# One hand-written order for four engines against another: hashed attention and a channel mix on one core

## The chip, the cores and the metric

The kernel runs on one core of a Trainium2 chip. The metric is the device time of one execution in microseconds (us). A core has engines that work side by side, each through its own list of instructions and strictly in the order of that list: TensorE (PE in the profile, with PEld for its weight loads), VectorE (DVE), ScalarE (ACT), GpSimd (POOL), and SyncE (SP), whose list here holds the DMA transfers.

## What is computed

The reference is attention followed by a channel mix. Queries and keys are sorted into buckets by the signs of six projections, and a query attends only to keys of its own bucket:

```python
mask = q_bucket[:, :, :, None] == k_bucket[:, :, None, :]
scores = np.where(mask, scale * np.matmul(q, k.transpose(0, 1, 3, 2)), -1000000000.0)
scores = scores - np.max(scores, axis=-1, keepdims=True)
attn = np.exp(scores)
attn = attn / (np.sum(attn, axis=-1, keepdims=True) + 1e-09)
x = np.matmul(attn, v)                      # 4 batches, 8 heads, 768 rows, 64 wide
# ---- then, with the heads side by side (512 wide), x_prev = x one row later ----
xk = mu_k * x + (1.0 - mu_k) * x_prev
xr = mu_r * x + (1.0 - mu_r) * x_prev
k = np.maximum(xk @ w_k, 0.0)               # 512 -> 1024
out = 1.0 / (1.0 + np.exp(-(xr @ w_r))) * (k * k @ w_v)
```

## The kernel before

The 32 heads are taken two at a time: 16 pairs, four to a batch. The work is cut into 1348 operations, each a closure of one to a few dozen instructions. They are added pair by pair in the loop at the end of the function, numbered from 0 to 1347 as they are added, and then issued in the order of a list of numbers, `ORDER`. Which of the eight banks of PSUM an operation writes is read from a second list, `BANKS`. So both the order on each engine and the place of each intermediate result are written out by hand; only the order within one engine counts, and each engine waits by semaphores for what its next operation needs.

```python
    def schedule(self):
        self.slot = dict(zip(self.names, BANKS))
        return [self.ops[i] for i in ORDER]
```

Operations are named below as the code names them, with n the pair (0 to 15), b the batch and c a chunk of 128 rows:

- `ldq`, `ldv` (SP, L328 and L333): load q and k, or v, of a pair. `wl` and `wc` (SP L297, POOL L304): load a piece of the weights and cast it to bf16.
- `hi`, `lo` (DVE, L396 and L399): split q and k into two fp16 halves; from pair 4 on, one operation each for q and k together. `tr` (SP, L403): a DMA transpose of that result into `a`. The first two pairs use PE transposes instead.
- `bits` (PE, L423), `bx` (DVE, L426), four `row` operations (POOL, L443, one for q and k of each head): bucket signs, made into +-64, copied into `a` as six more rows of the product, so that one matrix product gives score and mask.
- `sc` (PE, L566): nine score steps of 1024 columns for each pair, each in two PSUM banks; `exp` (ACT, L570) takes a step out of PSUM and frees the banks.
- `vsum`, three steps (POOL, L354, L357, L360), `mean` (PE, L372 and L373), two `va` and one `mc` (DVE, L378 and L385): v less its mean, from pair 4 on.
- `oo` (PE, L593): attention times v, two heads of three groups each; `rc` and `ob` (DVE, L604 to L611): divide by the row sum. `ot`, `xt` (PE L621, DVE L624) or `otd` (SP, L627, a DMA transpose): turn the result round.
- `xs`, `xz`, `df`, `xka`, `xk`, `xra`, `xr` (DVE, L631 to L666): shift by a row and mix.
- For each batch: `kp` (PE, L681, 16 products), `relu` (ACT, L685, into one of four buffers `kr`), `sq` (DVE, L688, the square, which frees the `kr` buffer); `r` (PE, L701) and `tanh` (ACT, L704); `v` (PE, L714, two halves), `os` (DVE, L721) and the store `st` (SP, L724).

A warm-up of 24 small products on PE (`warm`, L250) fills the start.

Of the kernel before, what the change touches and what calls it, by code (L numbers as in the profile page):

```python
# [17 lines left out]
    1, 27, 33, 34, 36, 35, 30, 74, 72, 75, 73, 76, 77, 0, 2, 31, 28, 3, 4, 5, 6, 38, 7, 37, 91, 81, 82, 85, 100, 8, 9, 10, 11, 12, 13, 14,  # L18
    15, 16, 101, 17, 92, 119, 26, 102, 93, 120, 110, 103, 86, 118, 104, 111, 94, 105, 95, 78, 96, 121, 18, 113, 122, 123, 127, 97, 106, 107,
    128, 129, 187, 79, 112, 124, 98, 108, 135, 114, 99, 158, 19, 125, 20, 134, 115, 109, 136, 159, 156, 143, 116, 117, 193, 144, 29, 32, 39,  # L20
    40, 41, 42, 43, 44, 45, 46, 47, 80, 87, 88, 83, 84, 130, 131, 189, 132, 133, 242, 137, 196, 194, 157, 126, 138, 197, 186, 240, 239, 198,
    145, 162, 154, 152, 163, 89, 146, 155, 153, 168, 169, 195, 190, 147, 141, 139, 90, 142, 191, 246, 150, 140, 151, 164, 165, 166, 148, 21,
    149, 167, 247, 249, 188, 160, 209, 250, 161, 219, 170, 213, 248, 210, 251, 171, 172, 214, 220, 292, 293, 50, 48, 199, 192, 243, 215,
    216, 173, 244, 174, 200, 203, 299, 201, 22, 221, 300, 207, 23, 24, 25, 217, 222, 208, 202, 175, 176, 177, 245, 204, 205, 218, 262, 252,
    206, 263, 301, 211, 253, 178, 179, 52, 241, 452, 453, 454, 442, 228, 212, 443, 266, 229, 264, 267, 294, 265, 258, 230, 272, 56, 259,
    295, 296, 255, 254, 257, 297, 256, 54, 58, 223, 224, 225, 226, 231, 273, 232, 260, 268, 261, 227, 269, 270, 180, 233, 271, 181, 182,
    308, 309, 302, 51, 183, 234, 303, 49, 184, 314, 318, 235, 320, 236, 238, 53, 315, 305, 274, 306, 298, 304, 321, 319, 276, 281, 277, 282,
    322, 445, 275, 446, 307, 278, 279, 316, 237, 455, 323, 312, 317, 280, 324, 313, 456, 507, 325, 508, 331, 463, 464, 465, 332, 310, 466,
    333, 283, 284, 461, 334, 469, 311, 285, 473, 185, 335, 462, 470, 286, 447, 458, 460, 326, 474, 509, 327, 448, 475, 287, 449, 328, 467,
# [12 lines left out]
    753, 755, 549, 834, 601, 422, 783, 867, 550, 551, 426, 772, 835, 832, 833, 427, 836, 837, 814, 428, 815, 784, 785, 786, 656, 787, 602,
# [759 lines left out]
```

## Time and profile before

| what | us |
|---|---|
| median of 3 runs | 246.14 |
| lowest, highest of them | 245.51, 246.46 |
| the execution that was profiled | 245.97 |
| its span, from the first to the last instruction | 244.2 |
| PE, DVE, ACT and POOL busy in that span | 233.6, 191.8, 183.4, 96.4 |

The times inside the profile count from the start of the span, so 1.8 us of the profiled execution lie outside it. PE's time to the end of a product is modelled and takes in the pipeline, so a busy PE isn't one at its peak. A timeline row gives start, duration, engine, line, operation, output and input, and how many instructions were merged; in square brackets stands how long the engine was idle before them and what it waited for.

### The profile page before, as it was taken

Reading aid. Unit: us, or ns where it says so; the run is one execution under the profiler, and the core shown is the slowest. Engines: PE = TensorE matmul, PEld = TensorE weight load, DVE = VectorE, ACT = ScalarE, POOL = GpSimd, SP = SyncE. Lnnn points to the kernel's source line nnn. Section 1 sums busy time; section 2 is a strip of 40 time slices with the busy share of each in tenths; the row PEclk is TensorE's granted clock in tenths of the full one; section 3 lists DMA queues with packets and bytes.
Section 4 is the critical chain, followed back from the end, with each engine's and each line's share of the span. In section 5 each row is a group of like instructions: output and inputs, shape, how many; then the busy total and the mean of one; then the engine's idle time right before and its main releaser. Section 6 shows DMA issues by size and latency. Waiting matters only on the chain.

```text
span 244.2 us, 6300 instructions
## 1 busy us (share of the span) xinstructions
PE 233.6 (96%) x2533; PEld 146.4 (60%) x2550; DVE 191.8 (79%) x396; ACT 183.4 (75%) x242; POOL 96.4 (39%) x152
## 2 busy tenths in 40 slices
PE   8999999998999998999999999999999999999994
PEld 6885666575667546456555765556565665455443
DVE  5879698999999999999898989992368168965332
ACT  4699999899998676878769996678797881265410
POOL 6248977985369563556076320500450000000000
PEclk9999999999999999999999999999999999999999
DMA  6999999999999998998999779409112210103133
GB/s 212 376 273 217 228 211 246 349 185 328 267 283 232 281 305 212 203 260 224 317 154 206 112 164 177 131 17 225 57 34 91 73 35 34 54 1 116 57 132 129
DMA packets 72526, 44.01 MB, mean 180 GB/s; under 512 B 54832, under 2 KB 67504, under 8 KB 72496
## 3 DMA queue, kind: packets, MB, share of 16 engines
q1 hardware_dynamic: 72272, 43.40, 74.6%
q8 instruction: 20, 0.33, 0.6%
q10 hardware_dynamic: 224, 0.20, 0.2%
q14 instruction: 10, 0.08, 0.1%
HBM read 24.12 MB, written 6.29 MB: 125 GB/s over the span
## 4 chain that ended last, share of the span: by engine, by line
PE 67%; DVE 12%; DMA 11%; ACT 4%; issue 3%; POOL 1%; DVEq 0%
PE ps_all L566 16%; PE ps_all L714 14%; PE ps_all L681 14%; DMA a<-nh 11%; PE ps_all L593 7%; PE ps_all L701 7%; ACT pt L570 3%; PE ps_all L423 3%; DVE k L688 2%; PE ps_all L250 2%; POOL a L443 1%; DVE ob L611 1%; DVE va L378 1%; DVE bx L426 1%; PE ps_all L489 1%
## 5 line engine op out<-in xcount | busy, mean ns | idle before, releaser
L570 ACT ACTIVATE pt<-ps_all 128x1024 bf16<-128x1024 f32 x144 | 140.2, 1037 | 14.9 <-PE ps_all L566 13.9
L566 PE MATMUL ps_all<-a 128*128 128x256 f16 (+1 forms) x384 | 81.1, 325 | 2.5 <-DVE mc L385 0.8
L443 POOL COPY a<-bx 6x384 f32<-6x384 f32 x56 | 42.6, 761 | 41.8 <-DVE bx L426 23.9
L681 PE MATMUL ps_all<-xk,wk 128*128 128x384 bf16 x256 | 50.1, 326 | 0.5 <-ACT kr L685 0.5
L566 PEld LDWEIGHTS <-a 128*128 128x128 f16 x384 | 33.8, 98 | 25.6 <-issue 6.3
L593 PEld LDWEIGHTS <-pt 128*128 128x128 bf16 x1152 | 43.2, 97 | 9.1 <-issue 1.4
L714 PE MATMUL ps_all<-wv,k 128*128 128x512 bf16 (+2 forms) x199 | 46.1, 362 | 0.6
L593 PE MATMUL ps_all<-va,pt 128*128 128x65 bf16 x1152 | 45.6, 193 | 0.0
L688 DVE TENSOR_TENSOR k<-kr 128x384 bf16<-128x384 bf16 x64 | 27.5, 453 | 13.1 <-ACT kr L685 12.9
L685 ACT ACTIVATE kr<-ps_all 128x384 bf16<-128x384 f32 x64 | 30.0, 502 | 9.5 <-PE ps_all L681 6.4
L681 PEld LDWEIGHTS <-wk 128*128 128x128 bf16 x256 | 23.8, 98 | 17.5 <-issue 1.7
L704 ACT ACTIVATE rs<-ps_all 128x512 f32<-128x512 f32 x24 | 14.1, 597 | 26.5 <-PE ps_all L701 11.2
L714 PEld LDWEIGHTS <-k 128*128 128x128 bf16 x208 | 19.4, 98 | 18.4
L399 DVE SCALAR_TENSOR_TENSOR nh<-nat,nh 128x1536 f16<-128x1536 f32 (+1 forms) x16 | 26.4, 1652 | 0.3
L721 DVE SCALAR_TENSOR_TENSOR os<-rs,ps_all 128x512 f32<-128x512 f32 (+2 forms) x26 | 16.7, 641 | 11.5 <-PE ps_all L714 8.1
L701 PE MATMUL ps_all<-wr,xr 128*128 128x512 bf16 x88 | 23.1, 379 | 0.4
L354 POOL TENSOR_TENSOR vt<-vn 128x384 f32<-128x384 f32 x12 | 15.1, 1256 | 16.1 <-DMA vn<-in_v_dram 15.5
L611 DVE TENSOR_TENSOR ob<-ps_all,rc 128x384 bf16<-128x384 f32 x32 | 17.3, 550 | 0.4
L426 DVE TENSOR_SCALAR bx<-ps_all 128x768 uint16<-128x768 uint16 x14 | 13.4, 954 | 3.9 <-PE ps_all L423 3.6
L701 PEld LDWEIGHTS <-xr 128*128 128x128 bf16 x96 | 9.2, 98 | 9.7 <-issue 0.3
L396 DVE TENSOR_SCALAR nh<-nat 128x1536 f16<-128x1536 f32 (+1 forms) x16 | 14.7, 924 | 0.3 <-DMA nat<-in_k_dram 0.3
L378 DVE SCALAR_TENSOR_TENSOR va<-ps_all,vn 128x384 bf16<-128x384 f32 x24 | 12.7, 548 | 1.5 <-ACT kr L685 0.8
(86 smaller groups left out, 191.1 us busy)
## 6 DMA issues: line engine op xcount, KB each, us to landing
vn<-in_v_dram SPq DMA_DIRECT2D x16, 384.0 KB, 5.5
out_dram<-os SPq DMA_DIRECT2D x23, 256.0 KB, 2.3
nat<-in_q_dram SPq DMA_DIRECT2D x15, 384.0 KB, 4.9
nat<-in_k_dram SPq DMA_DIRECT2D x15, 384.0 KB, 6.2
wst<-in_moe_w_k_dram SPq DMA_DIRECT2D x2, 512.0 KB, 6.1
wst<-in_moe_w_r_dram SPq DMA_DIRECT2D x2, 512.0 KB, 9.3
wst<-in_moe_w_v_dram SPq DMA_DIRECT2D x2, 512.0 KB, 5.4
k<-in_moe_w_k_dram SPq DMA_DIRECT2D x1, 512.0 KB, 6.3
```

The costliest lines, as they stand in the source:

```text
L399: nc.vector.scalar_tensor_tensor(out=nh[:, :, D:P], in0=nat.rearrange("p j (c d) -> p (j c) d", d=D), scalar=QS, in1=nh[:, :, 0:D], op0=AL ...
L443: nc.gpsimd.tensor_copy(side_a[side][sa][D : D + NB, j, :].bitcast(FP32), bx_t[sx][32 * i : 32 * i + NB, :].bitcast(FP32))
L566: nc.tensor.matmul(ps[:, lo - s * STEP : hi - s * STEP], side_a["k"][sa][:, j, jc * P : (jc + 1) * P], side_a["q"][sa][:, j, q0 : q0 + hi ...
L570: nc.scalar.activation(out=pt_t[sp][:, s * STEP : (s + 1) * STEP], in_=ps_t[plan.slot[nm]], func=AF.Exp, bias=EBIAS, scale=ESC)
L593: nc.tensor.matmul(oo[:, ic * 65 : ic * 65 + 65], pt_t[sp][:, o : o + P], va_t[sa][:, j, jc, 0 : D + 1], start=(not uc and ic == 0 and jc ...
L611: nc.vector.tensor_tensor(out=ob_t[so][:, :, j * D : (j + 1) * D], in0=oo[:, :, 0:D], in1=rc_t[sr][:, 1, :].unsqueeze(2).to_broadcast([P, ...
L681: nc.tensor.matmul(ps[:, 0:HALF], wk_sb[:, d, fc * P : (fc + 1) * P], xk_t[mx[d]][:, h * HALF : (h + 1) * HALF], start=(d == 0), stop=(d = ...
L685: nc.scalar.activation(out=kr_t[sk], in_=sm(nm)[:, 0:HALF], func=AF.Relu, scale=0.5 ** 0.5)
L688: nc.vector.tensor_tensor(out=k2_t[s2][:, h * HALF : (h + 1) * HALF], in0=kr_t[sk], in1=kr_t[sk], op=ALU.mult)
L701: nc.tensor.matmul(sm(nr), xr_t[mx[d]][:, c * P : (c + 1) * P], wr_sb[:, d, :], start=(d == 0), stop=(d == NDC - 1))
L714: nc.tensor.matmul(sm(nv)[:, x0:x1], k2_t[(b * NFC + fc) % NK2][:, c * P : (c + 1) * P], wv_sb[:, fc, x0:x1], start=(fc == 0), stop=(fc == ...
L721: nc.vector.scalar_tensor_tensor(out=os_t[so][:, x0:x1], in0=rs_t[s1][:, x0:x1], scalar=1.0, in1=sm(nv)[:, x0:x1], op0=ALU.add, op1=ALU.mult)
```

## The change

Both lists are replaced; no operation is added or taken away, and no shape, buffer or transfer changes. `ORDER` stays a list of the same 1348 numbers. Against the list before, 390 of PE's 475 operations stand at another place in PE's own order (by 2.9 places on average), 305 of 372 on DVE (4.8), 158 of 242 on ACT (1.6), 100 of 145 on POOL (2.1) and 69 of 114 on SP (1.2). Most of it begins with the third pair, but the first two pairs move a little as well, and so does SP's list. `BANKS` gives many results another PSUM bank. The first lines of the diff:

```diff
 ORDER = [
-    1, 27, 33, 34, 36, 35, 30, 74, 72, 75, 73, 76, 77, 0, 2, 31, 28, 3, 4, 5, 6, 38, 7, 37, 91, 81, 82, 85, 100, 8, 9, 10, 11, 12, 13, 14,
...
+    1, 27, 33, 34, 36, 35, 30, 31, 28, 29, 32, 39, 40, 74, 26, 0, 37, 38, 81, 100, 82, 85, 72, 41, 42, 43, 44, 45, 2, 3, 4, 5, 6, 7, 8, 9,
...
 BANKS = [
-    7, 4, 5, 6, 5, 1, 1, 2, 3, 6, 0, 0, 2, 2, 3, 1, 0, 0, 6, 0, 6, 1, 0, 2, 0, 1, 2, 1, 2, 2, 6, 7, 6, 0, 2, 0, 0, 2, 1, 1, 1, 2, 2, 7, 6,
...
+    7, 2, 5, 6, 4, 3, 3, 0, 2, 2, 6, 1, 3, 2, 6, 4, 5, 0, 6, 3, 6, 0, 1, 2, 0, 0, 2, 0, 2, 1, 6, 7, 1, 1, 0, 2, 1, 0, 0, 0, 1, 2, 1, 7, 6,
...
```

Numbers say little, so here are the stretches that the prediction speaks of, by name, in one engine's order (x2 and x3: so many in a row).

```
PE, pairs 2 to 4
before  sc2_2 bits3 sc1_3 oo1_1 sc2_4 oo1_1 sc2_3 sc2_0 oo1_1 sc2_7 oo1_0x3 sc2_1 sc2_5 sc2_6 ot0 ot1 sc3_0 bits4 sc3_3 sc3_5 sc3_6
        sc2_8 oo2_0 oo2_1 oo2_0 oo2_1 sc3_7 oo2_0 sc3_4 bits5 sc3_2 sc3_8 oo3_1 sc4_1
after   sc2_2 bits3 sc1_3 sc2_3 oo1_1x2 sc2_4 sc2_0 sc2_6 oo1_0x3 ot0 sc2_7 sc2_1 sc2_5 ot1 sc3_3 sc3_0 bits4 sc2_8 sc3_6 sc3_7
        oo2_0x3 sc3_5 oo2_1 sc3_4 oo2_1x2 sc3_8 sc3_2 bits5 sc4_1
POOL, pair 3
before  row3q1 row3q0 row3k1 vsum3b row3k0 wc0 row4q1 row4k0
after   row3q1 row3q0 vsum2c row3k1 row3k0 vsum3 vsum3b vsum3c row4k0
DVE, pairs 1 to 5 (mur, muk: two small operations on the mix weights)
before  hi5 lo5 rc1x2 ob1x2 xt0 xs0 mur df0 xt1 bx4 muk xk0 xs1 df1 xr1 rc2 xk1 ob2 bx5
after   hi5 lo5 rc1 xt0 ob1 muk ob1 mur xs0 df0 xt1 xr0 bx4 xs1 df1 xk1 rc2x2 ob2x2 xk0 bx5
SP, the eighth pair's transpose
before  tr7 wl7 wl8 otd4 ldq9k wl6 tr8
after   tr7 otd4 wl8 wl7 tr8 wl6 ldq9k
PE, around bits8
before  kp0_7_0 sc7_1 kp0_7_1 oo6_0 kp0_7_1 bits8 r0_0 sc7_6
after   r0_0 kp0_7_1x2 sc7_2 sc7_1 bits8 r0_1 sc7_6
DVE, behind bx8
before  bx8 xka4 hi9 lo9 xra4 sq0_7x2 sq0_6 va7 hi10 va7 os0_0_0 mc7 xr4 os0_1_0
after   bx8 sq0_6 sq0_7 hi9 lo9 va7x2 mc7 hi10 os0_0_0 xra4 os0_1_0          (the other sq0_7 stands ahead of bx8)
DVE, second batch
before  sq1_0 bx11 sq1_1 hi13 lo13 sq1_1 rc9 xr6 os0_5_0
after   sq1_0 sq1_1 sq1_0 mc9 rc9 ob9 sq1_2 xra6 os0_5_0 va10x2 hi13 mc10 sq1_3 lo13 sq1_1 sq1_2 rc9   (bx11 stands ahead)
PE, pair 12
before  bits12 oo9_0 sc11_5 kp1_5_0 sc10_7 oo9_0 sc11_7 mean11 oo9_0 kp1_6_0 sc11_3 oo10_0 sc11_6 oo10_0x2 oo10_1 kp1_4_1 sc11_8 oo10_1 sc12_4
after   bits12 sc10_8 oo10_0 sc11_7 oo10_0 mean11 sc11_3 oo10_0 kp1_6_0 sc11_6 kp1_4_1 oo10_1 sc12_4
DVE, pair 12
before  bx12 sq1_4 xra7 va11x2 sq1_2 mc11
after   bx12 hi14 va11 rc10 va11 xs8
POOL, the last pairs
before  vsum13b vsum13c row14q0 row14k1 row14q1 row14k0 row13k1 row13q1 vsum14 row15q1 vsum14b row15k1 row15q0 vsum14c vsum15 ...
after   vsum13b row13q1 row13k0 row13q0 vsum13c vsum14 vsum14b vsum14c vsum15 vsum15b row14k1 row14k0 row14q1 row14q0 row13k1 vsum15c row15q0 ...
SP, the last pairs
before  ... tr14 otd10 ldq15q ldq15k otd11 ldv15 st1_0_0 st1_2_0 st1_1_0 tr15 ldv14
after   ... ldq15q ldv14 otd9 tr14 otd10 st0_3_0 otd11 ldv15 st1_0_0 st1_2_0 tr15
PE, pairs 14 and 15
after   sc14_3 kp2_1_0 sc12_8 mean13 r1_4 kp2_1_1 sc14_2 v1_3_0 sc14_0 v1_3_0 sc13_5 oo12_1 sc13_8 oo12_1x2 sc14_5 sc14_6 mean15
        r1_5 kp2_3_0 sc13_4 v1_5_0 bits15 kp2_4_1 oo13_0 sc13_6
PE and DVE, the start
before  PE ... warm14 y0k0 warm15 y0q0 ...        DVE hi0q0 pw0 pw1 pwl0 hi0k0 ly0k0 pwl1 hi0k1
after   PE ... warm14 warm15 warm16 y0k0 y0q0 ... DVE pw0 hi0k0 pw1 pwl0 hi0k1 pwl1 hi0q0 ly0k0
```

(`y0k0` and `ly0k0` are the PE transpose of the first head's k and the step behind it, L481 and L499; `pw` and `pwl` prepare the projection, L732 and L738.)

116 rows, old and new, of tables (BANKS, ORDER) are left out of this document.

## The prediction, made before the result was known

> **What bounds the kernel now.** I read the page's busy times first, then the stretches of ten microseconds, and only then the timeline, at the places where PE or ACT stood still.
>
> ```profile
> span 244.2 us, 6300 instructions
> PE 233.6 (96%) x2533; PEld 146.4 (60%) x2550; DVE 191.8 (79%) x396; ACT 183.4 (75%) x242; POOL 96.4 (39%) x152
> 30.00:40.00 10.00, 9.41 (x140) 6.54 (x139) 8.71 (x15) 9.59 (x12) 7.24 (x9) 1.00 1.23 226
> 40.00:50.00 10.00, 8.91 (x145) 5.83 (x142) 9.90 (x14) 9.18 (x12) 8.37 (x9) 1.00 0.94 299
> 80.00:90.00 10.00, 9.60 (x85) 5.24 (x85) 9.90 (x15) 7.42 (x11) 5.48 (x8) 1.00 1.14 292
> 90.00:100.00 10.00, 8.91 (x119) 5.42 (x119) 9.29 (x19) 7.34 (x9) 3.40 (x5) 1.00 1.02 220
> 130.00:140.00 10.00, 10.00 (x153) 6.83 (x151) 8.91 (x24) 9.49 (x15) 4.76 (x9) 1.00 1.03 134
> 160.00:170.00 10.00, 9.95 (x70) 5.85 (x70) 5.86 (x13) 8.15 (x13) 0.00 (x0) 1.00 0.56 128
> ```
>
> (PE, PEld, DVE, ACT, POOL busy; then granted clock, DMA share, GB/s.) PE is the bound, and from 130 us on it is never idle for more than a trace: a new order can win nothing there and can only lose. What is to be won lies where PE is idle: 0.59 + 1.09 us in 30 to 50, and 0.40 + 1.09 us in 80 to 100. DVE is nearly full over the same stretches, so a gain on PE has to get past DVE as well.
>
> **The change, part by part.** Moves on PE are priced by the paced pieces of the chain of waits: a score step, a third of an `oo`, a `kp` and an `r` or half a `v`.
>
> ```profile
> 63.94 0.43 PE ps_all L566 x3
> 58.79 0.36 PE ps_all L593 x12
> 63.28 0.65 PE ps_all L681 x4
> 85.73 0.86 PE ps_all L701 x4
> ```
>
> *Start, 0 (between -0.2 and +0.45).* Two more warm-ups stand ahead of y0k0, and hi0k0, hi0k1 and hi0q0 ahead of ly0k0.
>
> ```profile
> 1.19 3.38 PE L250 MATMUL ps_all<-k 128*128 128x256 bf16 x15 [1.19 <-DVE k L247]
> 13.91 3.77 ACT L570 ACTIVATE pt<-ps_all 128x1024 bf16<-128x1024 f32 x4 [0.34 <-PE ps_all L566]
> ```
>
> Fifteen warm-ups take 3.38 us, so two cost 0.45 at most; DVE reaches ly0k0 some tenths later. But ACT waited for PE as late as 13.91, and PE reaches that step through the same chain of transposes, one of whose links (evt0k1 on ACT) now comes earlier. I take nothing.
>
> *30 to 50 us, -1.0 (between -1.5 and +0.3).* Here ACT sets the pace.
>
> ```profile
> 36.61 0.83 PE L423 MATMUL ps_all<-a,p 128*32 128x512 f16 x16 [0.34 <-DMA a<-nh]
> 38.08 5.61 ACT L570 ACTIVATE pt<-ps_all 128x1024 bf16<-128x1024 f32 x6 [0.41 <-PE ps_all L566]
> 43.10 0.83 PE L423 MATMUL ps_all<-a,p 128*32 128x512 f16 x16 [0.77 <-DMA a<-nh]
> 44.51 12.14 ACT L570 ACTIVATE pt<-ps_all 128x1024 bf16<-128x1024 f32 x13 [0.82 <-PE ps_all L566]
> ```
>
> bits4 and bits5 stand in PE's list waiting for their transposes to land, the score steps behind them wait too, and ACT runs dry: 0.41 + 0.82 = 1.23 us. In the new list one score step more stands ahead of bits4 (sc3_3 and sc3_0), and sc3_8 and sc3_2 ahead of bits5. An exp comes every 12.14 / 13 = 0.93 us, so ACT has 0.93 and 1.87 us more work in hand: enough to cover both waits if the transposes land as before (tr4 and tr5 keep their places on SP). What is late next: ot1 now waits for ob1, which stands behind xt0, and bx4 behind xr0, so PE may stand 0.3 us at sc3_3 and as much for the bank that bx4 frees. And the first-batch products need xk3:
>
> ```profile
> 58.95 1.18 DVE L657 SCALAR_TENSOR_TENSOR xk<-df,muk,xt 128x768 bf16<-128x768 bf16 x1
> 60.27 0.32 PE L681 MATMUL ps_all<-xk,wk 128*128 128x384 bf16 x1
> ```
>
> PE took it 0.14 us after it was ready (60.13). In the new list the first product that needs it stands 1.2 us later on PE, so that a gain of about 1.2 us passes. I take 1.0.
>
> *bits8, -0.35 (between -0.35 and 0).* tr8 went out behind ldq9k and wl6; now it goes first.
>
> ```profile
> 71.45 7.73 SPq L403 DMA_TRANSPOSE a<-nh  x1
> 82.62 0.83 PE L423 MATMUL ps_all<-a,p 128*32 128x512 f16 x16 [0.35 <-DMA a<-nh]
> DMA to landing us min/median/max: 4.4/5.9/11.1
> ```
>
> It was the slowest transpose: 82.6 - 71.45 = 11.1 us to its landing. Its source lo8 stands 1.7 us of work later on DVE, so it can't go out much before 71.45, but bits8 stands 1.3 us later on PE as well (r0_0 0.86 and sc7_2 0.43 have moved ahead of it). The wait of 0.35 goes either way; no more is to be won there.
>
> *80 to 100 us, -1.0 (between -1.14 and 0).* 1.49 us of idle PE, less the 0.35 above.
>
> ```profile
> 88.68 2.31 DVE L688 TENSOR_TENSOR k<-kr 128x384 bf16<-128x384 bf16 x3
> 91.38 0.94 DVE L396 TENSOR_SCALAR nh<-nat 128x1536 f16<-128x1536 f32 x1
> 93.30 0.15 DVE L385 TENSOR_SCALAR mc<-ps_all 128x1 f32<-128x1 f32 x1
> 93.50 0.59 PE L566 MATMUL ps_all<-a 128*128 128x256 f16 x3 [0.78 <-DVE mc L385]
> ```
>
> PE waited 0.78 us for the bank that mc7 frees, and mc7 stood behind hi10 and os0_0. Now sq0_7 and sq0_6 come ahead of hi9 and lo9, and mc7 ahead of hi10; the 0.94 of hi10 no longer stands between, nor do the three squares (2.31) stand behind lo9. What is late next is os0_0, which waits for PE itself. I take 1.0.
>
> *128 us, -0.3 (between -0.51 and 0).* PE waited for relu, relu for a `kr` buffer, and the square that frees it stood behind lo13:
>
> ```profile
> 124.58 1.93 DVE L399 SCALAR_TENSOR_TENSOR nh<-nat,nh 128x1536 f16<-128x1536 f32 x1
> 128.22 0.81 PE L681 MATMUL ps_all<-xk,wk 128*128 128x384 bf16 x4 [0.51 <-ACT kr L685]
> ```
>
> One sq1_1 still stands behind lo13, but PE needs that buffer later; most of it goes.
>
> *After 130 us, +0.5 (between 0 and +4.2).* Every cushion that shrinks counts here; the rivals price the two thinnest. I put 0.5 for small waits: between mean15 and the oo13_0 that needs ob12's bank PE has 0.86 + 0.65 + 0.43 + 0.86 + 0.76 + 0.65 = 4.2 us of work, and DVE ten short operations of about 0.43 each, 4.3 us.
>
> *Other queues and banks, 0.* The stores and loads on SP change places by one or two, except ldv14 and ldq15k (10 and 9 earlier, into stretches where the DMA share falls) and st0_3 (5 later, its buffer is next written by the second batch). The new banks add the waits named above.
>
> **Sum.** 0 - 1.0 - 0.35 - 1.0 - 0.3 + 0.5 = -2.15 us. From the profiled execution's 245.97 that is 243.8; the median of the runs, 246.14, lies 0.17 above that execution, so I say 243.9.
>
> **Rivals.** *(1) Slower: vsum15 blocks row14.* POOL now sums v of the last pair ahead of pair 14's rows, and PE's sc14_3 needs the fourth of them.
>
> ```profile
> 152.32 0.54 SPq L333 DMA_DIRECT2D vn<-in_v_dram  x1
> DMA to landing us min/median/max: 3.4/5.5/9.1
> L354 POOL TENSOR_TENSOR vt<-vn 128x384 f32<-128x384 f32 x12 | 15.1, 1256 | 16.1 <-DMA vn<-in_v_dram 15.5
> L357 POOL TENSOR_TENSOR vt<-vt 128x128 f32<-128x128 f32 x12 | 6.9, 572 | 1.0
> L443 POOL COPY a<-bx 6x384 f32<-6x384 f32 x56 | 42.6, 761 | 41.8 <-DVE bx L426 23.9
> 165.85 0.60 PE L566 MATMUL ps_all<-a 128*128 128x512 f16 x3
> ```
>
> ldv15 still stands behind otd11 on SP, which waits for ob11, so that it goes out at 152.32 as before. With a median landing row14 is done at 152.32 + 5.5 + 1.26 + 0.57 + 4 x 0.76 = 162.7; PE, at 165.85 before, comes there 1.4 us earlier in its list and with 2.65 us won, at 161.8: a wait of 0.9, or none with the shortest rows, and 0.5 is in the sum for this. With the slowest landing row14 is done at 166.3, a wait of 4.5 and a time of 245.97 - 2.65 + 4.5 = 247.8; rows of 1.27 us (rival 3) make the same from a landing of 7.1 on. It begins to cost from a landing of some 4.6 us, and eats the whole gain at about 7.2. For it: POOL sat idle behind such a load before. Against: DMA is light by then. *(2) The gain stops at DVE.* DVE is 87 to 99% busy in the stretches quoted up to 140; if its waits don't shrink with PE's, the early microseconds come back as waits for DVE: 246.0. Against: DVE's own idle waits go as well. *(3) Rows beside hi14.* Between bits12 and sc12_4, which needs all four rows, PE's work shrinks from 8.2 to 5.3 us, and hi14 now follows bx12 at once.
>
> ```profile
> 130.31 0.83 PE L423 MATMUL ps_all<-a,p 128*32 128x512 f16 x16
> 132.38 2.34 POOL L443 COPY a<-bx 6x384 f32<-6x384 f32 x4 [1.66 <-issue]
> 30.72 3.82 POOL L443 COPY a<-bx 6x384 f32<-6x384 f32 x3
> 31.68 1.94 DVE L399 SCALAR_TENSOR_TENSOR nh<-nat,nh 128x1536 f16<-128x1536 f32 x1
> ```
>
> Before, the rows ended 134.72 - 130.31 = 4.4 us after bits12 began. Beside lo5 three rows took 3.82, 1.27 each; four of those would make 7.1 and a wait of 1.8: 245.6. The Trainium skill's GPSIMD Engine Reference, section "Specifications", says that GpSimd shares its SBUF interfaces with VectorE and meets contention from instructions in a two-port mode or with two SBUF inputs; the rows beside lo5 agree. Against: hi14 lasts 0.95 us, not four rows. *(4) More:* all the waits named go and nothing comes in the late half: 245.97 - 1.5 - 0.35 - 1.14 - 0.51 = 242.5.
>
> **Chances.** What a measurement of this kernel tells from no change is about 0.5%, 1.23 us: faster means under 244.9, slower over 247.4. Forecast (243.0 to 244.9) 0.47; rival 4, 0.08; rival 2, 0.12; rival 3, 0.08; rival 1 at its far end (247.4 or more) 0.25, given high since PE has no idle time left in the late half, so that whatever lands late there shows in full. So faster 0.55, same 0.20, slower 0.25. The range takes all but the far end of rival 1 and of rival 4: 242.0 to 248.0; the likeliest case alone 243.0 to 244.9.
>
> **What would show it.** Right: no wait of PE for `a<-nh` over 0.2 us at bits4, bits5 and bits8; ACT without a gap of 0.3 us between 18 and 50; no PE wait for mc near 93; bits9 at about 95.8 (98.2 before). Wrong: PE idle at sc14_3 for POOL while POOL waits for vn, or at sc12_4; idle of over 1 us for DVE between 60 and 130; or a start that puts ACT's unbroken run from 18 us on later by 0.3 or more.

## The result and the profile after

| | before | after |
|---|---|---|
| median of 22 runs each, us | 246.72 | 247.83 |
| lowest, highest | 245.51, 248.22 | 246.66, 249.08 |
| the profiled execution, its span | 245.97, 244.2 | 247.19, 245.4 |

The ratio after to before is 1.0041, with a 95% interval from 1.0023 to 1.0058: the changed order is 0.41% slower, 1.0 us (1.1 between the medians), where 0.9% faster was forecast. Both profiled executions lie some 0.7 us below the median of their kernel, so a wait that is read in one of them needn't be typical.

The page's busy line and the stretches of ten microseconds, after (PE, PEld, DVE, ACT, POOL busy, granted clock, DMA share, GB/s):

```profile
span 245.4 us, 6293 instructions
PE 234.5 (96%) x2531; PEld 146.2 (60%) x2550; DVE 190.5 (78%) x396; ACT 182.5 (74%) x242; POOL 97.8 (40%) x152
...
30.00:40.00 10.00, 9.51 (x123) 6.01 (x122) 9.67 (x18) 9.85 (x12) 6.38 (x9) 1.00 1.22 241
40.00:50.00 10.00, 10.00 (x172) 7.03 (x171) 8.84 (x13) 9.82 (x11) 7.59 (x9) 1.00 0.87 298
60.00:70.00 10.00, 8.18 (x70) 4.90 (x69) 9.46 (x12) 7.50 (x13) 8.32 (x8) 1.00 0.93 260
80.00:90.00 10.00, 9.95 (x99) 5.73 (x98) 8.92 (x20) 8.70 (x12) 7.06 (x10) 1.00 1.12 330
90.00:100.00 10.00, 9.51 (x122) 5.82 (x122) 9.68 (x18) 8.08 (x9) 5.74 (x7) 1.00 0.87 178
130.00:140.00 10.00, 10.00 (x153) 6.86 (x151) 9.65 (x22) 9.22 (x14) 4.90 (x8) 1.00 1.08 279
```

Where the forecast sought its microseconds they came: 40 to 50 went from 8.91 busy to 10.00, 80 to 90 from 9.60 to 9.95, 90 to 100 from 8.91 to 9.51. But a stretch for which its sum has no term, 60 to 70, went from 10.00 to 8.18. There the kernel before had been full on PE, and nearly so on VectorE:

```profile
60.00:70.00 10.00, 10.00 (x94) 6.45 (x93) 9.53 (x16) 9.76 (x16) 4.93 (x6) 1.00 1.17 271
70.00:80.00 10.00, 10.00 (x163) 6.96 (x161) 9.75 (x25) 8.98 (x13) 7.78 (x9) 1.00 1.11 265
```

ACT's timeline after, from the first scores on:

```profile
13.98 4.94 ACT L570 ACTIVATE pt<-ps_all 128x1024 bf16<-128x1024 f32 x5 [0.34 <-PE ps_all L566]
19.64 5.72 ACT L570 ACTIVATE pt<-ps_all 128x1024 bf16<-128x1024 f32 x6 [0.72 <-PE ps_all L566]
25.55 4.78 ACT L570 ACTIVATE pt<-ps_all 128x1024 bf16<-128x1024 f32 x5 [0.19 <-PE ps_all L566]
30.48 15.77 ACT L570 ACTIVATE pt<-ps_all 128x1024 bf16<-128x1024 f32 x17 [0.15 <-PE ps_all L566]
```

The gaps of 0.41 and 0.82 at 38 and 44.5 us are gone; in their place stand 0.72, 0.19 and 0.15 before 31 us. And here is the hole, on PE, with VectorE's list beside it:

```profile
66.59 0.38 PE L566 MATMUL ps_all<-a 128*128 128x512 f16 x1
68.55 0.38 PE L566 MATMUL ps_all<-a 128*128 128x512 f16 x1 [1.58 <-DVE mc L385]
```

```profile
62.64 1.93 DVE L399 SCALAR_TENSOR_TENSOR nh<-nat,nh 128x1536 f16<-128x1536 f32 x1
64.50 1.01 DVE L378 SCALAR_TENSOR_TENSOR va<-ps_all,vn 128x384 bf16<-128x384 f32 x2
65.43 1.91 DVE L688 TENSOR_TENSOR k<-kr 128x384 bf16<-128x384 bf16 x2
67.27 1.17 DVE L396 TENSOR_SCALAR nh<-nat 128x1536 f16<-128x1536 f32 x1
68.35 0.15 DVE L385 TENSOR_SCALAR mc<-ps_all 128x1 f32<-128x1 f32 x1
68.42 1.07 DVE L688 TENSOR_TENSOR k<-kr 128x384 bf16<-128x384 bf16 x2
```

The two rows of PE are the two halves of score step sc6_7. `BANKS` now puts it in banks 6 and 7, where it stood in 2 and 3 before. Bank 7 holds mean5 until mc5 has read it, and mc5 stands behind va5, the squares sq0_1 and hi8. In the kernel before, the same squares (sq0_0, sq0_1) stood ahead of va5 and hi8; VectorE waited for ACT there, and the squares were short:

```profile
63.09 0.36 DVE L688 TENSOR_TENSOR k<-kr 128x384 bf16<-128x384 bf16 x1
63.85 0.90 DVE L688 TENSOR_TENSOR k<-kr 128x384 bf16<-128x384 bf16 x3 [0.41 <-ACT kr L685]
```

### The profile page after: what moved, and what is told of

It is laid out like the page before. It is cut to its first block, busy times and chain, and to the rows that moved or that the text cites. A ratio compares the mean times of both kernels' runs of the same rounds, so it can differ in the third digit from the quotient of the medians.

```text
span 245.4 us, 6293 instructions
## 1 busy us (share of the span) xinstructions
PE 234.5 (96%) x2531; PEld 146.2 (60%) x2550; DVE 190.5 (78%) x396; ACT 182.5 (74%) x242; POOL 97.8 (40%) x152
## 4 chain that ended last, share of the span: by engine, by line
PE 50%; DVE 3%; ACT 2%; issue 1%; DVEq 0%; ACTq 0%
PE ps_all L714 14%; PE ps_all L681 11%; PE ps_all L566 10%; PE ps_all L701 6%; PE ps_all L593 6%; PE ps_all L423 2%; ACT pt L570 1%; DVE k L688 1%; ACT kr L685 1%; DVE bx L426 1%; DVE va L378 1%; DVE tm L663 0%; DVE ob L611 0%; DVE xr L666 0%; DVE df L652 0%
## 5 line engine op out<-in xcount | busy, mean ns | idle before, releaser
L443 POOL COPY a<-bx 6x384 f32<-6x384 f32 x56 | 43.5, 777 | 50.2 <-DVE bx L426 31.8
L681 PE MATMUL ps_all<-xk,wk 128*128 128x384 bf16 x256 | 49.4, 326 | 0.5 <-DVE mc L385 0.2
L714 PE MATMUL ps_all<-wv,k 128*128 128x512 bf16 (+2 forms) x201 | 45.4, 362 | 0.5
L593 PE MATMUL ps_all<-va,pt 128*128 128x65 bf16 x1152 | 44.8, 193 | 0.3
L688 DVE TENSOR_TENSOR k<-kr 128x384 bf16<-128x384 bf16 x64 | 26.0, 428 | 12.0 <-ACT kr L685 11.7
L399 DVE SCALAR_TENSOR_TENSOR nh<-nat,nh 128x1536 f16<-128x1536 f32 (+1 forms) x16 | 27.1, 1694 | 0.2
L354 POOL TENSOR_TENSOR vt<-vn 128x384 f32<-128x384 f32 x12 | 12.3, 1026 | 14.1 <-DMA vn<-in_v_dram 13.3
L396 DVE TENSOR_SCALAR nh<-nat 128x1536 f16<-128x1536 f32 (+1 forms) x16 | 16.0, 1003 | 1.1 <-DMA nat<-in_q_dram 0.9
```

The costliest lines, as they stand in the source:

```text
L399: nc.vector.scalar_tensor_tensor(out=nh[:, :, D:P], in0=nat.rearrange("p j (c d) -> p (j c) d", d=D), scalar=QS, in1=nh[:, :, 0:D], op0=AL ...
L443: nc.gpsimd.tensor_copy(side_a[side][sa][D : D + NB, j, :].bitcast(FP32), bx_t[sx][32 * i : 32 * i + NB, :].bitcast(FP32))
L593: nc.tensor.matmul(oo[:, ic * 65 : ic * 65 + 65], pt_t[sp][:, o : o + P], va_t[sa][:, j, jc, 0 : D + 1], start=(not uc and ic == 0 and jc ...
L681: nc.tensor.matmul(ps[:, 0:HALF], wk_sb[:, d, fc * P : (fc + 1) * P], xk_t[mx[d]][:, h * HALF : (h + 1) * HALF], start=(d == 0), stop=(d = ...
L688: nc.vector.tensor_tensor(out=k2_t[s2][:, h * HALF : (h + 1) * HALF], in0=kr_t[sk], in1=kr_t[sk], op=ALU.mult)
L714: nc.tensor.matmul(sm(nv)[:, x0:x1], k2_t[(b * NFC + fc) % NK2][:, c * P : (c + 1) * P], wv_sb[:, fc, x0:x1], start=(fc == 0), stop=(fc == ...
```

## The experiments

Orders are given by name, on one engine. Each ratio is to the kernel before, in runs on the same chip, with its 95% interval.

**1. The bank alone.** mc5 is moved on VectorE, in the changed order.

```diff
  lo7 va5 va5
+ mc5
  sq0_1 sq0_1 hi8
- mc5
  sq0_0 sq0_0
```

> The changed order with one DVE instruction moved: mc5 directly behind va5, ahead of the two sq0_1 and hi8, everything else as changed. Theory (the changed order wins its early microseconds and loses 1.58 of them where sc6_7 waits at 66.8 us for the bank that mc5 frees): mc5 would end at about 65.65, before PE asks for the bank at 66.4, so that the idle time goes, less 0.15 that the squares and hi8 come later: 1.3 to 1.5 us less than the changed kernel, which was 1.0 over the kernel before, so 0.2 to 0.6 us below the kernel before. Rival (VectorE's amount of work sets the pace between 60 and 130 us, and the wait for mc5 is only where it shows): PE waits for another VectorE result instead within the next ten microseconds, and the time stays 0.8 to 1.2 us over the kernel before.

Measured: 1.0037 (1.0010 to 1.0065), as slow as the changed kernel. PE and ACT in this kernel:

```profile
59.33 0.65 PE L681 MATMUL ps_all<-xk,wk 128*128 128x384 bf16 x3 [0.52 <-DVE ob L611]
61.52 0.59 PE L566 MATMUL ps_all<-a 128*128 128x512 f16 x2 [0.61 <-DVE bx L426]
68.94 0.65 PE L681 MATMUL ps_all<-xk,wk 128*128 128x384 bf16 x3 [0.79 <-ACT kr L685]
```

```profile
65.98 0.55 ACT L685 ACTIVATE kr<-ps_all 128x384 bf16<-128x384 f32 x1
68.40 0.49 ACT L685 ACTIVATE kr<-ps_all 128x384 bf16<-128x384 f32 x1 [1.87 <-DVE k L688]
```

My first theory fell. The wait for mc is gone, and behind it stands another: relu waited 1.87 us for a square to free its buffer, and PE 0.79 for relu. The waits for ob and bx in the first two rows belong to work that VectorE does ahead of mc5 in both orders, so the move can't have made them. What can be compared is PE's time from the start of sc6_6 to that of sc6_1, where its list is the same: 9.39 us in the trace of the changed kernel, 9.33 in this one. The longest wait of a trace had a second one hidden behind it, and what the move saved was gone within ten microseconds.

**2. The squares too.** VectorE's order between lo7 and sq0_2, in the changed order.

```diff
  lo7
+ sq0_1 sq0_1 va5 va5 mc5 sq0_0 sq0_0 hi8
- va5 va5 sq0_1 sq0_1 hi8 mc5 sq0_0 sq0_0
```

> The changed order with VectorE's order mended between 62 and 70 us: after lo7 come sq0_1, sq0_1, va5, va5, mc5, sq0_0, sq0_0 and then hi8 (changed order: va5, va5, sq0_1, sq0_1, hi8, mc5, sq0_0, sq0_0); all else as changed. With mc5 alone moved ahead the time stayed, and PE's wait of 1.58 for mc5 came back as 0.79 for kr at 68.9, since relu0_3 waited 1.87 us for a square. Theory (the order on VectorE decides here: the squares, which free the buffers that relu needs, stand behind va5 and hi8): relu0_3 comes 1 us sooner, and the time falls by 0.8 to 1.3 us from the changed kernel, to within 0.4 us of the kernel before. Rival (VectorE has simply too much to do up to here, whatever comes first): the wait moves on to bits8's or lo8's users, and the time stays 0.8 to 1.2 us over the kernel before.

Measured: 1.0002 (0.9976 to 1.0028). The loss is gone, as the theory had it, though the interval still overlaps the end of the changed kernel's (from 1.0023 on). From sc6_6 to sc6_1 PE takes 8.42 us in this trace, 0.97 less than in the changed kernel, and its wait for mc5 has shrunk from 1.58 us to this:

```profile
67.43 0.38 PE L566 MATMUL ps_all<-a 128*128 128x512 f16 x1 [0.19 <-DVE mc L385]
```

**3. The squares alone.** Only the two sq0_1 go ahead of va5.

```diff
  lo7
+ sq0_1 sq0_1
  va5 va5
- sq0_1 sq0_1
  hi8 mc5 sq0_0 sq0_0
```

> The changed order with the two sq0_1 ahead of va5 on VectorE, hi8 and mc5 where the changed order has them; all else as changed. With mc5 alone moved the time stayed 0.9 us over the kernel before; with both moved it equalled it. Theory (two waits side by side at 66 to 69 us, PE's for mc5's bank and relu's for the square, each enough by itself): PE still waits 1.3 to 1.6 us for mc5 at sc6_7, and the time stays 0.7 to 1.2 us over the kernel before. Rival (the squares alone decide, the wait for the bank shrinks by as much as they come sooner): within 0.4 us of the kernel before.

Measured: 1.0002 (0.9977 to 1.0027), though the median of its 12 runs, 247.24, lies 0.58 over that of the kernel before. The trace still has PE waiting for mc5:

```profile
68.42 0.38 PE L566 MATMUL ps_all<-a 128*128 128x512 f16 x1 [1.05 <-DVE mc L385]
```

The ratio speaks for the rival, the row for a part of the theory. From sc6_6 to sc6_1 PE takes 8.87 us here. So of the 0.97 us that 2 saves in this stretch the two sq0_1 bring 0.52, and mc5 and the two sq0_0 ahead of hi8 bring the other 0.45, while mc5 moved by itself (1) brings next to nothing. These are single traces, so the sizes are rough.

**4. The same delay in the kernel before.** hi8 goes ahead of the squares.

```diff
  lo7
+ hi8
  rc4 sq0_0 sq0_1 sq0_1 sq0_0 ob4
- hi8
  sq0_2
```

> The kernel before with one VectorE instruction moved: hi8 directly behind lo7, ahead of rc4, the four squares sq0_0 and sq0_1, and ob4 (before: behind them); all else as before. It gives the kernel before the delay that the changed order gives the squares, alone: 1.0 to 1.5 us. Theory (those squares are the link by which VectorE holds PE here: relu waits for their buffers, PE for relu): ACT waits for k, PE for kr or for relu's banks, and the time rises by 0.6 to 1.3 us. Rival (the squares have slack in the order before): within 0.3 us.

Measured: 1.0053 (1.0027 to 1.0078), 1.3 us. ACT and PE in it:

```profile
65.88 0.49 ACT L685 ACTIVATE kr<-ps_all 128x384 bf16<-128x384 f32 x1 [0.24 <-DVE k L688]
66.98 0.87 ACT L685 ACTIVATE kr<-ps_all 128x384 bf16<-128x384 f32 x2 [0.61 <-DVE k L688]
```

```profile
67.38 0.59 PE L566 MATMUL ps_all<-a 128*128 128x512 f16 x2 [0.32 <-DVE ob L611]
```

ACT waits for the squares, as the theory had it, 0.85 us in all. PE's first wait here is for ob4, though, which stands behind hi8 as well, so this run prices the squares and ob4 together. Undone in the changed kernel (2) and brought into the other (4), the order of a few VectorE instructions at this place moves the time by about 1 us. That is the cause of the slowdown, shown from both sides.

**5. bits4 and bits5 alone.** The forecast's largest term, on PE in the kernel before.

```diff
+ sc3_0 sc3_3 bits4 ... sc3_4 sc3_2 sc3_8 bits5
- sc3_0 bits4 sc3_3 ... sc3_4 bits5 sc3_2 sc3_8
```

> The kernel before with two moves on PE alone: bits4 one score step later (behind sc3_3) and bits5 two score steps later (behind sc3_2 and sc3_8), as in the changed order; VectorE, ScalarE, GpSimd, queues and banks as before. Theory (the waits of ScalarE at 38 and 44.5 us come from these two and the gain is kept to the end): ACT runs without its gaps of 0.41 and 0.82, and the time falls by 0.7 to 1.2 us. Rival (VectorE sets the pace behind it: bx4 and bx5 come later, and the lead is given back as waits for VectorE by 80 us): the gaps go, and the time changes by less than 0.3 us.

Measured: 1.0074 (1.0048 to 1.0101), 1.8 us slower, which neither theory had. VectorE, ACT and PE in it:

```profile
39.29 0.96 DVE L426 TENSOR_SCALAR bx<-ps_all 128x768 uint16<-128x768 uint16 x1 [1.32 <-PE ps_all L423]
46.65 0.96 DVE L426 TENSOR_SCALAR bx<-ps_all 128x768 uint16<-128x768 uint16 x1 [0.39 <-POOL a L443]
```

```profile
47.67 6.52 ACT L570 ACTIVATE pt<-ps_all 128x1024 bf16<-128x1024 f32 x7 [0.74 <-PE ps_all L566]
```

```profile
37.76 0.59 PE L566 MATMUL ps_all<-a 128*128 128x512 f16 x3 [0.71 <-ACT pt L570]
```

VectorE, in order, now stands still behind bx4 until bits4 is done. And PE waits ahead of the moved sc3_3 for a bank that an exp has to free: the banks are still those of the list before, in which sc3_3 stood behind bits4. To test the first of the two, the same moves with work of VectorE put there, as the changed order has it:

```diff
  PE as above; DVE:  df0 xt1
+ muk xr0
  bx4 ...
```

> The kernel before with bits4 and bits5 moved on PE as in the experiment that was 1.8 us slower, and with one more move on VectorE, as in the changed order: muk's copy and xr0 ahead of bx4. In that experiment VectorE stood idle 1.32 us for bits4 with bx4 at its head. Theory (the moved bits cost because VectorE, in order, stands still behind bx4, and the changed order pays nothing since it has put xr0 there): VectorE's idle time there falls by about 1.0, the time is 0.5 to 1.1 us over the kernel before, not 1.8. Rival (the loss comes from the rows of pairs 4 and 5 on GpSimd, which come later whatever VectorE does meanwhile): 1.5 to 2.2 us over.

Measured: 1.0031 (1.0007 to 1.0056), 0.8 us over. The stop at bx4 is gone (bx4 at 39.45 with no idle ahead of it), and by the ratios a little over half of the loss with it. But VectorE now stops at bx5, where it had waited 0.39:

```profile
46.81 0.96 DVE L426 TENSOR_SCALAR bx<-ps_all 128x768 uint16<-128x768 uint16 x1 [1.42 <-PE ps_all L423]
```

PE's wait for the exp ahead of sc3_3 is there again as well, 0.72 us. So VectorE's stop at bx4 is likely a part of the loss; what the old banks cost was not tested, and the rest stays open. A wait that is moved later on one engine can come back as a longer one on the next.

**6. mc7 alone.** VectorE only, in the kernel before.

```diff
  bx8 xka4
+ sq0_7 sq0_7 sq0_6 hi9 lo9 xra4 va7 va7 mc7 hi10 os0_0_0
- hi9 lo9 xra4 sq0_7 sq0_7 sq0_6 va7 hi10 va7 os0_0_0 mc7
```

> The kernel before with moves on VectorE alone, as in the changed order: the three squares sq0_7, sq0_7, sq0_6 ahead of hi9, and both va7 and mc7 ahead of hi10; all else as before. Theory: mc7 ends some 1.5 us sooner, PE's wait of 0.78 near 93 us goes and stays away, the time falls by 0.5 to 0.8 us. Rival (the waits only move: hi9, lo9 and hi10 come 1 to 2 us later, and with them their transposes, or xr4 and os0 on VectorE): less than 0.2 us, or slower.

Measured: 0.9970 (0.9941 to 1.0000), 0.7 us less (0.5 between the medians): the term of 80 to 100 us stands by itself, as the theory had it, though the interval ends at no change. PE's 8.91 in 90 to 100 became:

```profile
90.00:100.00 10.00, 9.47 (x122) 5.75 (x122) 9.41 (x19) 8.03 (x9) 4.44 (x7) 1.00 1.04 192
```

**7. sq1_1 ahead of lo13, on top of 6.**

```diff
  hi13
+ sq1_1
  lo13
- sq1_1
  rc9 xr6
```

> The kernel before with the VectorE moves of the mc7 experiment (squares ahead of hi9, va7 and mc7 ahead of hi10; 0.5 to 0.7 us below the kernel before) and one more: sq1_1 directly ahead of lo13, which in the profile of before stands 1.93 us ahead of it while relu, and PE behind relu, wait for the buffer that it frees. Theory (both waits are PE's own and go for good): PE's wait for kr at 128 us goes, another 0.3 to 0.5 us, in all 0.9 to 1.1 us below the kernel before. Rival (lo13 and with it tr13 and bits13 come later, and PE waits there): no more than with mc7 alone, 0.4 to 0.7 us below.

Measured: 0.9984 (0.9959 to 1.0008), no better than 6. The wait for kr at 128 us went, and this came:

```profile
129.72 0.81 PE L681 MATMUL ps_all<-xk,wk 128*128 128x384 bf16 x4 [0.71 <-DVE ob L611]
```

ob9 stands behind lo13 as well, so the wait passed from one result of VectorE to the next, not to bits13, as the rival had it.

**8. Splices.** Up to an operation in one order, from there in the other, banks along with it.

```diff
 ORDER = [
+    the first 776 of before (123 us), the rest as after
+    the first 484 of before (73 us), the rest as after
+    the first 405 of after (60 us), the rest as before
+    the first 304 of after (44.6 us), the rest as before
+    the first 484 of before, up to 859 (137 us) as after, the rest as before
 ]
```

> Spliced: the kernel before up to about 123 us (its first 776 operations in its own order), then the rest in the changed order. In the profiles PE's idle time beyond its paced work grows from 131 us to the end by 0.54 us in the kernel before and by 1.37 in the changed one, in many small waits of 0.2 to 0.45. Theory (the changed order loses 0.8 us in its second half by itself): 0.5 to 1.0 us over the kernel before. Rival (the small waits come from what the first half hands over, not from the order of the second): within 0.2 us of the kernel before, or below it by the 0.2 to 0.3 of the wait at 128 us that the changed order removes.

> Spliced: the kernel before up to about 73 us (its first 484 operations), then the rest in the changed order. In the six profiles so far PE's idle time from 73 us on is 3.9 to 4.0 us in the order before and 3.0 to 3.3 in the changed one. Theory (the changed order loses only between 55 and 75 us and wins 0.7 from 80 on): 0.4 to 0.9 us below the kernel before. Rival (what the first part hands over decides, and the changed rest needs the changed front): within 0.3 us of the kernel before, or slower.

> Spliced: the changed order up to about 60 us (its first 405 operations), then the rest in the order before. Theory (the changed order wins nothing up to 55 us that counts, since in executions whose start is 0.3 to 1.1 us later than the profiled one bits4 and bits5 hardly wait, and its loss lies behind 60 us): within 0.4 us of the kernel before. Rival A (the loss was made before 60 us, on VectorE, where xr3, rc4 and ob4 come earlier, and only shows behind it): 0.7 to 1.3 us over the kernel before. Rival B (my forecast's 1.0 us of gain in 30 to 50 us is there): 0.6 to 1.0 us below.

> Spliced: the changed order up to about 44.6 us (304 operations, bits5 the last on PE), then the order before. The splice at 60 us was 2.5 us slower than the kernel before. Theory (those 2.5 are VectorE work pulled ahead between 45 and 60 us, xr3, rc4, ob4, and squares that then come too late; the start of the changed order costs 0.5 and its moved bits win as much): within 0.5 us of the kernel before. Rival A (the loss is in the start and the moves of bits4 and bits5, as in the kernel before with those two alone moved, 1.8 us slower): 1.0 to 2.0 us over. Rival B (the forecast's gain in 30 to 50 us is there, the start costs nothing): 0.7 to 1.1 us below.

> Spliced twice: the kernel before up to about 73 us (484 operations), the changed order from there to about 137 us (to operation 859), then the order before to the end. In the profiles so far PE's idle time from 73 to 137 us of the kernel before is 3.5 us in the order before and 2.0 to 2.4 in the changed one, and from 137 us to the end 0.4 us in the order before and 1.0 to 1.2 in the changed one. Theory (the changed order is better in the middle alone): 1.0 to 1.5 us below the kernel before. Rival (what the middle wins is taken back by whatever comes behind it, as it seems to be in the splice at 73 us, whose median equals the kernel before): within 0.4 us.

Measured: 0.9990 (0.9967 to 1.0013), 1.0002 (0.9976 to 1.0027), 1.0106 (1.0071 to 1.0141), 1.0079 (1.0049 to 1.0109) and 1.0012 (0.9985 to 1.0038). The end of the changed order, alone, costs nothing that can be measured, against the theory. Nor does its middle win anything that can be measured, against the theory of both splices that have it. In the traces, by the measure that the next section explains, PE loses 3.3 us in 80 to 131 us of its work in the kernel before, 2.3 in the splice at 73 us and 2.8 in the last one; why nothing of that shows in the runs I can't resolve. The changed front is dear when the old rest follows it: 2.6 us at 60, more than any expectation had, and 1.9 at 44.6, within rival A's range. In the splice at 44.6 us it is a seam, though: xr1, which only the old order puts there, stands ahead of bx5, and PE waits for that bank.

```profile
45.85 1.25 DVE L657 SCALAR_TENSOR_TENSOR xr<-df,mur,xt 128x768 bf16<-128x768 bf16 x1
47.02 0.94 DVE L426 TENSOR_SCALAR bx<-ps_all 128x768 uint16<-128x768 uint16 x1
```

```profile
48.12 1.03 PE L566 MATMUL ps_all<-a 128*128 128x512 f16 x5 [2.08 <-DVE bx L426]
```

The splice at 60 us has waits of 0.26 for bx, 0.52 for ACT and 0.58 for kr between 61 and 70 us, and no single place. Its squares stand ahead of va5 and hi8, as in the kernel before, and yet ACT waits 1.20 us for them at 68.33: behind the changed front the old order of the squares does not mend the stretch, as that of 2 does. These two price the fit between two orders; I draw nothing from them about the front by itself.

**9. Less work on GpSimd.** The sums of v, in each of the two orders.

```diff
+ F = E if uc else 1
- e.tensor_tensor(out=vt[:, :, :, 0:E], in0=src[:, :, 0:3, 0:E], in1=src[:, :, 3:6, 0:E], op=ALU.add)
+ e.tensor_tensor(out=vt[:, :, :, 0:F], in0=src[:, :, 0:3, 0:F], in1=src[:, :, 3:6, 0:F], op=ALU.add)
- e.tensor_tensor(out=vt[:, :, 0, 0:E], in0=vt[:, :, 0, 0:E], in1=vt[:, :, 1, 0:E], op=ALU.add)
+ e.tensor_tensor(out=vt[:, :, 0, 0:F], in0=vt[:, :, 0, 0:F], in1=vt[:, :, 1, 0:F], op=ALU.add)
```

> The kernel before with most of GpSimd's sums of v left out from pair 4 on: the first two of the three additions of each pair work on one column in place of 64, so that the column means are not those of the reference; their instructions, waits and places stay. Takes 15 to 20 us of work off GpSimd, in pieces of 1.3 and 0.5, beside which VectorE's bf16 and f16 instructions are stretched. Theory (VectorE, stretched by GpSimd, sets PE's pace from 40 to 120 us): VectorE's busy time falls by 3 to 7 us, and the time by 0.8 to 2.5 us. Rival (PE waits for VectorE only through the order, VectorE's amount of work doesn't matter): the busy time falls and the time changes by less than 0.4 us.

> The changed kernel with the same cut of GpSimd's sums of v as in the experiment on the kernel before (the first two additions of each pair from pair 4 on work on one column, so that the column means are not the reference's). That one was 2.9 us below the kernel before. Theory (the changed order's loss is VectorE's crowding between 62 and 70 us, where sums, casts and rows on GpSimd stretch it): the loss of 1.0 goes or shrinks to under 0.4, so 2.5 to 3.3 us below the kernel before. Rival (the order is late by itself, the squares stand behind va5 and hi8 whatever they last): 1.6 to 2.2 us below the kernel before.

Measured: 0.9883 (0.9853 to 0.9913) in the order before, 2.9 us less; 0.9970 (0.9943 to 0.9997) in the changed one. The page's busy line of the first, and the group of squares before and in it (busy us, mean ns, idle before; two lines were added, so L688 is L690):

```profile
PE 235.1 (97%) x2550; PEld 147.0 (60%) x2550; DVE 186.5 (77%) x396; ACT 183.3 (75%) x242; POOL 80.1 (33%) x152
```

```profile
L688 DVE TENSOR_TENSOR k<-kr 128x384 bf16<-128x384 bf16 x64 | 27.5, 453 | 13.1 <-ACT kr L685 12.9
```

```profile
L690 DVE TENSOR_TENSOR k<-kr 128x384 bf16<-128x384 bf16 x64 | 24.1, 400 | 13.3 <-ACT kr L687 13.2
```

GpSimd does 16.3 us less, VectorE's busy time falls by 5.3 although none of its work was taken away, 3.4 of it in the squares, and the time falls by 2.9. So the rival fell, and the gain is larger than the theory's 0.8 to 2.5. Either the time that VectorE takes paced PE before, or GpSimd's rows and sums did, which come earlier too; the run doesn't separate the two. In the changed order the theory fell, and the rival's number (1.6 to 2.2 below) didn't come either: it is 0.7 us below the kernel before. Its loss against the order before, with the sums left out in both, is 2.1 us where it had been 1.0, from runs on two chips with intervals of some 0.7 us either way. PE still waits for mc5.

```profile
67.56 0.38 PE L568 MATMUL ps_all<-a 128*128 128x512 f16 x1 [1.01 <-DVE mc L387]
```

By the measure of the next section, one trace each, the changed order now loses 1.3 us more than the order before between 50 and 80 us of PE's work, where it had lost 1.9 more; behind 80 us it loses 1.1 more, where it had lost 0.5 less. So most of the loss between 50 and 80 us is an order that is late, and crowding made at most a third of it. What grew lies behind 80 us, where PE waits 1.04 us for a bx at 102.8, and is another loss.

**10. Versions meant to be faster.** The changed order as in 2 up to 137 us, then the order before; the same with the second ob3 ahead of xs2 and the first ob1 ahead of xt0; and the kernel of 6 with two casts on ACT.

```diff
+ the first 859 operations in the order of 2, the rest as before
+ DVE:  ... ob1 xt0 ...  xr1 rc3 ob3 ob3 xs2 ...
- DVE:  ... xt0 ob1 ...  xr1 rc3 ob3 xs2 ob3 ...
- W_CAST = ["POOL"] * 10
+ W_CAST = ["ACT" if i in (6, 9) else "POOL" for i in range(10)]
```

> The changed order with the squares mended between 62 and 70 us, up to about 137 us (to operation 859), then the order before to the end. Theory (the small waits of the changed order behind 137 us cost 0.5 to 0.8 us, and all its other parts together come out even with the kernel before): 0.4 to 1.0 us below the kernel before. Rival (PE's small waits there come from what is handed over): within 0.3 us.

> The changed order with the squares mended and its last part from the order before (as in the run that came out 0.4 us below the kernel before), and two VectorE moves more: the second ob3 ahead of xs2, and the first ob1 ahead of xt0. PE's transposes of ob3 waited 1.3 to 1.5 us for that ob3 in the two traces of the mended order, 0.2 to 0.3 in others, and those of ob1 0.2. Theory (each is a wait of PE alone, so that what goes there stays gone): another 0.5 to 0.9 us, in all 0.8 to 1.3 us below the kernel before. Rival (ACT, which waits for the step behind, is the only thing helped, and is not the bound by then): 0.2 to 0.5 us below the kernel before.

> The kernel before with the mc7 moves (0.5 to 0.7 us below the kernel before) and two of the ten weight casts, wc6 and wc9, on ACT in place of GpSimd: wc6 behind the last relu0_7, wc9 behind tanh0_1, where ACT stood idle 1.1 us each for PE. Takes 2.2 us of work off GpSimd between 81 and 89 us. Theory (less on GpSimd makes VectorE faster, about 0.18 us for each us by the run with the cut sums): another 0.2 to 0.5 us, in all 0.7 to 1.2 us below the kernel before. Rival (the casts end ACT's idle time too late, and the exps of pair 7 behind them come later by some tenths): 0 to 0.4 us below.

Measured: 0.9985 (0.9962 to 1.0007), 0.9996 (0.9974 to 1.0018) and 0.9976 (0.9947 to 1.0005), that is 0.4, 0.1 and 0.6 us below the kernel before. The first and the third lie between their theories and rivals, and the second falls short of both. None has a lower ratio than 6, which at 0.9970 stays the lowest of the kernels that compute all of the reference; the intervals overlap, so the runs don't rank these four.

## Why the prediction was wrong, step by step

To set executions side by side I took, for each trace, the time at which PE began a piece of work, less the work that it had done by then at the prediction's paced durations, and its growth over four stretches of that work, in us:

| PE's own work | order before | changed order |
|---|---|---|
| 12 to 28 us | 1.81 (1.39 to 2.16, 10 executions) | 2.35 (1.99 to 2.59, 8) |
| 28 to 50 | 4.31 (3.74 to 5.15, 8) | 3.51 (2.82 to 4.12, 7) |
| 50 to 80 | 0.91 (0.79 to 1.06, 5) | 2.79 (2.63 and 2.94); squares mended 1.25, 1.25 and 1.69 |
| 80 to 210 | 3.94 (3.86 to 4.00, 6) | 3.05 (2.96 to 3.28, 4) |

The differences, +0.54 - 0.80 + 1.88 - 0.89, make +0.7, near the 1.0 that the ratio gives. The table leaves out the first 12 us of work and what lies behind 210. The split between its first two rows isn't firm: with every border one microsecond of work earlier, their differences come out as +0.36 and -0.62, with the same sum of -0.26. The third and fourth rows hold.

- **Start, 0: too low, by at most half a microsecond.** The link that I named, ACT's wait for PE, is where it shows: 0.72 + 0.19 + 0.15 idle before 31 us. The warm-ups were not it. sc0_7 waits for the step that takes q's transpose out of PSUM, which stands behind hi3, and sc1_8 for bx2. Both come from the new banks: that transpose now lies in bank 4, one of the two of sc0_7, and bits2 in banks 2 and 3, as sc1_8; in the list before neither pair shared a bank.

```profile
19.01 1.54 PE L566 MATMUL ps_all<-a 128*128 128x512 f16 x7 [0.46 <-DVE a L539]
...
24.92 0.59 PE L566 MATMUL ps_all<-a 128*128 128x256 f16 x3 [0.29 <-DVE bx L426]
```

- **30 to 50, -1.0: the waits went, the gain was too large.** There is no wait for `a<-nh` at bits4 or bits5 in any of nine traces of the changed front. But the prediction took the waits of one execution for the kernel's. In eight traces of the order before, all with the same instructions up to here, the two sum to 1.11, 0.61, 0, 0, 0.76, 0.43, 1.64 and 1.33: 0.74 in the mean. And the two moves alone lost 1.8 us (5): the gain, if any, hung on the rest of the new order, VectorE's for one, which I hadn't priced.
- **bits8, -0.35, and 80 to 100, -1.0: right mechanism, somewhat too large.** PE waits neither for bits8's transpose nor for mc7; from 80 to 210 us the changed order loses 0.89 less, where the terms from here on make 1.15, and mc7 alone is worth 0.7 by the ratio (6).
- **128 us, -0.3: the wait went, the gain didn't stay** (7).
- **After 130, +0.5: in the right place and harmless.** The splice at 123 us, which has the changed end, is at 0.9990.
- **"Other queues and banks, 0": the step that failed.** It said that "the new banks add the waits named above". I had looked at new banks and moved operations where the profile before was idle, and not between 60 and 80 us, where PE was full and VectorE 95 to 98% busy. There sq0_1 fell behind two va5, sq0_0 behind hi8 as well, and sc6_7 came upon bank 7; no other term covers VectorE's order there. So the term that stood at 0 is a loss of 1.9 us between 50 and 80 us, and with VectorE's order mended there (2) the slowdown is gone.
- **Rivals.** vsum15 (1) did not block: PE has no wait at sc14_3, though vsum15 came late, after 8.94 us of idle GpSimd:

```profile
156.89 1.00 POOL L354 TENSOR_TENSOR vt<-vn 128x384 f32<-128x384 f32 x1 [8.94 <-DMA vn<-in_v_dram]
```

  Nor did the rows beside hi14 (3). Rival 2, the gain that stops at VectorE, was the nearest, but it expected given-back waits; what came was a new one larger than the gains.
- **What would show it.** Of the signs named in advance, "idle of over 1 us for DVE between 60 and 130" came, 1.58 us at 68.55, and so did a late run of ACT, at 19.64 where it had been 17.90. bits9 began at 98.69, not at 95.8.
- **The range.** The measured 247.83 lies inside 242.0 to 248.0, and close to the 247.8 that rival 1 gave for the slowest landing. Rival 1's mechanism was not at work, so that is luck. In the sum, 246.14 - 2.15 is 244.0, not 243.9.

## What to carry to other kernels

A reordering is judged where the profile is full, not only where it is idle: list, for each engine near 95%, which results another engine waits for and what now stands ahead of each, banks included. Behind the longest wait look for the second, which ends soon after; an experiment that removes one of them may show nothing. And before a wait of a few tenths of a microsecond is entered in a sum, see whether it is there in a second execution.

## What the runs showed of the hardware

Executions of one instruction list differ by more than this change moves the median (245.53 to 249.17 in one set of 30 of the kernel before), and one thing that differs between them is which of VectorE and GpSimd comes first. Here are two traces whose instructions are the same up to this point, that of the changed kernel and that of experiment 2, each with VectorE's xr1 and the weight cast on GpSimd beside it:

```profile
51.24 1.10 DVE L657 SCALAR_TENSOR_TENSOR xr<-df,mur,xt 128x768 bf16<-128x768 bf16 x1
```

```profile
51.46 1.77 POOL L304 CAST wk<-wst 128x1024 bf16<-128x1024 f32 x1
```

```profile
50.78 1.68 DVE L657 SCALAR_TENSOR_TENSOR xr<-df,mur,xt 128x768 bf16<-128x768 bf16 x1
```

```profile
50.61 1.03 POOL L304 CAST wk<-wst 128x1024 bf16<-128x1024 f32 x1
```

Whichever begins first keeps its short time (1.10, 1.03), and the other stretches by 0.6 to 0.7. In experiment 2 GpSimd came first by 0.17 us; xr1, and the copy xs2 behind it in the same way, held up the second ob3 to 53.89 where it had begun at 53.20. PE, itself 0.5 us earlier in that execution, waited for it:

```profile
54.50 0.51 PE L621 MATMUL ps_all<-idb,ob 128*128 128x128 bf16 x6 [1.32 <-DVE ob L611]
```

```profile
53.80 0.51 PE L621 MATMUL ps_all<-idb,ob 128*128 128x128 bf16 x6 [0.17 <-DVE ob L611]
```

The Trainium skill, page "SBUF — State Buffer", section "Who interferes with whom", says that VectorE and GpSimd share a pair of ports, that a VectorE instruction with two inputs in SBUF, as xr1 has, contends with a GpSimd instruction that reads SBUF, and, of two-port modes, that the one that issues first holds the pair for its whole instruction while the other blocks. The traces agree on who is late; but the two overlap by 0.9 us in each trace and the stretch is 0.6 to 0.7, so they don't show that the second stands still throughout. In the changed kernel GpSimd had waited 0.47 us for a load:

```profile
50.52 1.00 POOL L354 TENSOR_TENSOR vt<-vn 128x384 f32<-128x384 f32 x1 [0.47 <-DMA vn<-in_v_dram]
```

Without that wait the cast would have begun at about 50.99 (an estimate, 51.46 - 0.47), ahead of xr1. So some tenths of a transfer's landing can decide which of the two engines is late, and an order found with one set of landings meets another in the next execution.
